# A gated mix of a long convolution and a shifted MLP: a new order of the steps behind the first 232, with new evacuation engines and ring buffers

## The chip, the cores and the metric

The kernel runs on one core of one Trainium2 chip. The metric is device time in microseconds. A core has TensorE (PE, with its weight loads shown apart as PEld), VectorE (DVE), ScalarE (ACT), GpSimd (POOL) and SyncE (SP), which here issues nearly all DMAs. Each engine works through its own queue in program order and waits on semaphores for the others.

## What is computed

S = 2048 positions of D = 640 channels, F = 1536. Cut to what matters:

```python
g = sigmoid((x * gate_w).sum(-1, keepdims=True))          # x = A_q
k_shift = sum over t < 4 of k_pad[:, t:t+S, :] * shift_k[:, 3-t]
kv = k_shift * v
y = irfft(rfft(kv, 2S) * rfft(ssm_k, 2S))[:S] + kv * ssm_D  # along the positions
a = x * y
h = gelu(layernorm(x) @ w1)
hs = shifted(h) @ w2        # four quarters of the channels shifted by 1, -1, 2, -2 positions
x1 = x + hs
b = x1 + gelu(layernorm(x1) @ w3) @ w4
return g * a + (1 - g) * b
```

## The kernel before, in words

The convolution is a two-stage Fourier transform on TensorE. **step1** (L423) multiplies kv (KV) and the filter (HT0) by a 64-point table; its PSUM banks are cast into a staging tile stg (L360 on ACT, L362 on DVE) and stored to DRAM scratch S_x (for kv) and S_h (for the filter). **gather** (L444) loads blocks of either, regrouped, into tiles ax. **step2** (L465) does the 32-point stage into XS and hs, **product** multiplies the spectra on DVE, **step3** (L512) transforms back into gs, stored to S_g (L523), **gin** loads it regrouped (L537), and **step4** (L893) does the last stage, with the gate and q applied (L897 to L907).

The MLP: **mlp1** (L707) into HT with gelu on ACT; **h_shift** on POOL; **w2** (L788), two PSUM banks of 320 columns for each of 16 tiles of positions, added to X on DVE (L791), with a square sum on ACT (L797); **x1_norm** normalizes four tiles into xn (L662 on ACT, L664 on DVE) and transposes them by DMA into x1t (L821); **w3** (L840) with gelu into gt (L844); **w4** (L867), added to X on DVE (L870); **store** (L855).

Steps are generators or lists of small pieces. The table ORDER names the 1099 pieces in the sequence in which they are emitted, "step1.HT0.2.VAVAAAAAAA:4" being piece 4 of step1 for block 2 of HT0; its letters say which evacuation goes to ACT (A) and which to DVE (V). Nothing else reorders the work, so ORDER sets each engine's queue. Tiles of a ring come from SLOTS: one digit for each tile in the order of allocation, saying which buffer it gets ("c": the 8 PSUM banks; "row": four buffers of 4 x 640 that stg, xn, gs, kn and q2 share; "ax": four for gather; "hp": four for hs). A new tile waits until everything that read its buffer's last tile is done, a DMA too.

Pieces that are tiled use a part of TensorE's rows or columns per matmul (step1, step2, step3, the gate); mlp1, w2, w3, w4 and step4 use all of them.

Of the kernel before, what the change touches and what calls it, by code (L numbers as in the profile page):

```python
# [41 lines left out]
def kernel(  # L42
# [24 lines left out]
        "c": "012345670124703510347205142356401723605162370514731057423671045261304732641374153670421350627413"  # L67
             "502634751264351270361427503164257364102546173045621537426107432715604371401362570164301257613045"
             "267236057416537621507362651374026372401534762501373150427102547535706432073125640736450750634127"
             "504763270415367204325170635147630125460327156034215760147362304167135620316425031672301402715320"  # L70
             "1724107361761423564023714053627501267420674256271306234",
# [807 lines left out]
    def step4(t1, ev):  # L879
# [32 lines left out]
        "open.L1.left:0 "  # L912
        "open.A2.right:0 "
        "consts0:0 "
        "load_x0.0:0 "
        "warm:0 "
        "load_x0.1:0 "
        "consts0:1 "
        "warm:1 "
        "warm:2 "  # L920
        "pow0:0 "
        "kv_alloc:0 "
        "k_load.3.AVA:0 "
        "f4_table:0 "
        "x_stats.0.VVVA:0 "
        "warm:3 "
        "k_load.3.AVA:1 "
        "x_stats.0.VVVA:1 "
        "load_x.1:0 "
        "x_stats.0.VVVA:2 "  # L930
        "k_load.3.AVA:5 "
        "x_stats.0.VVVA:3 "
        "x_stats.0.VVVA:4 "
        "x_stats.0.VVVA:5 "
        "x_stats.0.VVVA:6 "
        "warm:4 "
        "row_order:0 "
        "k_load.2.VAV:0 "
        "f1_table:0 "
        "x_norm.0.VVAA:0 "  # L940
        "x_norm.0.VVAA:1 "
        "f4_table:1 "
        "x_stats.1.VVVV:0 "
        "k_load.3.AVA:2 "
        "load_x.3:0 "
        "x_norm.0.VVAA:2 "
        "x_stats.1.VVVV:1 "
        "k_load.3.AVA:3 "
        "x_turn.0.AAA:0 "
        "k_load.3.AVA:6 "  # L950
        "k_load.2.VAV:5 "
        "load_w1.1:0 "
        "x_norm.0.VVAA:3 "
        "k_load.2.VAV:1 "
        "x_stats.1.VVVV:2 "
        "x_turn.0.AAA:1 "
        "x_stats.1.VVVV:3 "
        "x_turn.0.AAA:2 "
        "x_stats.1.VVVV:4 "
        "load_w1.0:0 "  # L960
        "x_stats.1.VVVV:5 "
        "x_stats.3.VVAA:0 "
        "k_load.3.AVA:4 "
        "x_norm.1.VVVV:0 "
        "x_turn.0.AAA:4 "
        "k_load.2.VAV:3 "
        "x_turn.0.AAA:3 "
        "x_turn.0.AAA:5 "
        "x_stats.3.VVAA:1 "
        "x_norm.1.VVVV:1 "  # L970
        "x_norm.1.VVVV:2 "
        "v_load.2:0 "
        "k_load.0.AAV:0 "
        "f1_table:1 "
        "mlp1.0.2:0 "
        "mlp1.0.3:0 "
        "x_norm.1.VVVV:3 "
        "v_load.0:0 "
        "k_load.1.AVV:0 "
        "k_load.2.VAV:6 "  # L980
        "mlp1.0.0:0 "
        "load_x.2:0 "
        "x_stats.3.VVAA:2 "
        "x_turn.1.VVV:0 "
        "x_turn.1.VVV:4 "
        "mlp1.0.1:0 "
        "x_stats.3.VVAA:3 "
        "x_turn.1.VVV:1 "
        "k_load.2.VAV:4 "
        "x_stats.3.VVAA:4 "  # L990
        "x_stats.3.VVAA:5 "
        "k_load.0.AAV:3 "
        "x_turn.1.VVV:5 "
        "mlp1.0.3:1 "
        "x_stats.3.VVAA:6 "
        "x_turn.1.VVV:2 "
        "v_load.3:0 "
        "x_turn.1.VVV:3 "
        "k_load.1.AVV:3 "
        "w1_mixed:0 "  # L1000
        "v_load.1:0 "
        "mlp1.0.0:1 "
        "x_stats.2.VVAA:0 "
        "mlp1.0.2:1 "
# [84 lines left out]
        "mlp1.3.3:0 "
        "tap.0.AVAA:3 "  # L1090
        "h_shift.0:2 "
        "tap.0.AVAA:5 "
        "tap.2.AVAA:8 "
        "h_shift.3:1 "
        "mlp1.3.2:0 "
        "tap.0.AVAA:4 "
        "tap.2.AVAA:6 "
        "tap.0.AVAA:1 "
        "mlp1.3.3:1 "
        "tap.0.AVAA:6 "  # L1100
        "tap.1.VAVA:0 "
        "tap.0.AVAA:7 "
        "tap.1.VAVA:5 "
        "tap.1.VAVA:1 "
        "tap.2.AVAA:4 "
        "mlp1.3.2:1 "
        "load_h.1:0 "
        "mlp1.2.2:0 "
        "tap.0.AVAA:8 "
        "tap.2.AVAA:1 "  # L1110
        "tap.1.VAVA:7 "
        "h_shift.1:1 "
        "tap.0.AVAA:2 "
        "load_h.3:0 "
        "mlp1.2.3:0 "
        "tap.1.VAVA:2 "
        "tap.1.VAVA:3 "
        "tap.2.AVAA:2 "
        "step1.KV.3.AAAVAVAAAV:9 "
        "tap.1.VAVA:8 "  # L1120
        "tap.1.VAVA:6 "
        "mlp1.2.2:1 "
        "mlp1.2.3:1 "
        "tap.1.VAVA:4 "
        "step1.KV.3.AAAVAVAAAV:11 "
        "step1.KV.3.AAAVAVAAAV:3 "
        "step1.KV.3.AAAVAVAAAV:10 "
        "step1.KV.3.AAAVAVAAAV:12 "
        "h_shift.0:3 "
        "step1.KV.3.AAAVAVAAAV:13 "  # L1130
        "step1.KV.3.AAAVAVAAAV:5 "
        "mlp1.2.4:0 "
        "step1.KV.3.AAAVAVAAAV:6 "
        "load_h.4:0 "
        "step1.KV.3.AAAVAVAAAV:0 "
        "step1.KV.3.AAAVAVAAAV:4 "
        "step1.KV.3.AAAVAVAAAV:14 "
        "h_shift.1:2 "
        "step1.KV.2.AVAVAVAAAA:6 "
        "z_rows:0 "  # L1140
        "z_rows:1 "
        "step1.KV.3.AAAVAVAAAV:2 "
        "step1.KV.3.AAAVAVAAAV:7 "
        "load_h.0:0 "
        "step1.KV.1.VAVAAAVVAA:0 "
        "step1.KV.3.AAAVAVAAAV:8 "
        "step1.KV.2.AVAVAVAAAA:8 "
        "step1.KV.3.AAAVAVAAAV:1 "
        "step1.KV.2.AVAVAVAAAA:3 "
        "z_rows:2 "  # L1150
        "mlp1.2.1:0 "
        "mlp1.2.1:1 "
        "h_shift.3:2 "
        "step1.KV.3.AAAVAVAAAV:16 "
        "step1.KV.1.VAVAAAVVAA:1 "
        "step1.KV.3.AAAVAVAAAV:15 "
        "mlp1.2.0:0 "
        "h_transpose.0.VV:2 "
        "step1.KV.2.AVAVAVAAAA:5 "
# [905 lines left out]
```

## Time and profile before

| | us |
|---|---|
| median of 3 runs (lowest to highest) | 227.55 (227.49 to 231.56) |
| the profiled execution | 227.13 |
| its span | 225.4 |
| PE busy | 217.8 (97%) |
| DVE busy | 183.7 (81%) |
| ACT busy | 171.4 (76%) |
| POOL busy | 38.1 (17%) |

The span is what the profiler saw of one execution; 1.7 us of the execution's time lie outside it. Busy matmuls overlap, since they are pipelined, so a matmul's own duration in the profile is longer than its share of the stream; the chain that ended last counts each stretch of time once. The granted clock is 1.00 in all stretches.

### The profile page before, as it was taken

How to read it: one execution, taken by the hardware profiler on the slowest of the kernel's cores; microseconds unless marked ns; L12 is line 12 of the kernel's file. 1: busy time of each engine (PE TensorE's matmuls, PEld its weight loads, DVE VectorE, ACT ScalarE, POOL GpSimd, SP SyncE). 2: the span in 40 equal slices, each digit the busy share in tenths (PEclk: the TensorE clock that was granted, in tenths of full speed). 3: DMA queues.
4: the chain of work that ended last, by engine and by line, in shares of the span. 5: the costliest groups of instructions: out<-in, count | busy, mean ns of one | idle time of the engine just before them, and what ended most of it. 6: DMA issues, size and time to landing. Idle time of an engine off the chain costs nothing.

```text
span 225.4 us, 6053 instructions
## 1 busy us (share of the span) xinstructions
PE 217.8 (97%) x2427; PEld 121.5 (54%) x2428; DVE 183.7 (81%) x447; ACT 171.4 (76%) x341; POOL 38.1 (17%) x91
## 2 busy tenths in 40 slices
PE   8989999899999999999999999999999999999994
PEld 2557455447846563345664444556533547657762
DVE  7898998868889969963899988989999841439994
ACT  4899988787999999999987597967988450266450
POOL 4247246816000431300600000000000000000000
PEclk9999999999999999999999999999999999999999
DMA  6999998892998999999989570690794879429914
GB/s 226 374 376 344 258 280 170 317 364 107 361 365 355 348 295 265 410 334 343 254 219 338 116 243 0 191 379 17 119 305 166 249 259 366 175 60 305 324 70 179
DMA packets 41770, 57.61 MB, mean 256 GB/s; under 512 B 18446, under 2 KB 34446, under 8 KB 41486
## 3 DMA queue, kind: packets, MB, share of 16 engines
q1 hardware_dynamic: 41166, 54.60, 75.4%
q0 software_dynamic: 576, 2.62, 3.1%
q8 instruction: 19, 0.31, 0.6%
q14 instruction: 9, 0.07, 0.1%
HBM read 34.93 MB, written 18.35 MB: 236 GB/s over the span
## 4 chain that ended last, share of the span: by engine, by line
PE 79%; DMA 9%; DVE 4%; ACT 4%; issue 1%; POOL 1%; SPq 0%; ACTq 0%
PE ps L840 24%; PE ps L867 23%; PE psw L788 7%; PE ps L465 5%; PE ps L893 4%; DMA X<-in_A_q_dram 4%; PE psm L707 4%; DMA xt<-xn 3%; PE psz L228 3%; PE ps L512 3%; PE ps L423 2%; PE pst L390 2%; DVE X L791 2%; ACT stg L360 2%; DMA S_x<-stg 2%; PE psk L590 1%
## 5 line engine op out<-in xcount | busy, mean ns | idle before, releaser
L840 PE MATMUL ps<-x1t,W 128*128 128x512 bf16 x240 | 56.1, 380 | 0.1
L867 PE MATMUL ps<-W,gt 128*128 128x320 bf16 (+2 forms) x383 | 55.1, 299 | 0.1
L867 PEld LDWEIGHTS <-gt 128*128 128x128 bf16 x384 | 36.2, 98 | 17.7 <-issue 3.0
L844 ACT ACTIVATE gt<-ps 128x512 bf16<-128x512 f32 x48 | 27.6, 609 | 19.0 <-PE ps L867 10.6
L840 PEld LDWEIGHTS <-W 128*128 128x128 bf16 x240 | 21.9, 98 | 28.7 <-issue 5.9
L360 ACT CAST stg<-ps 128x512 bf16<-128x512 f32 x55 | 28.6, 604 | 2.3 <-PE ps L423 2.0
L870 DVE SCALAR_TENSOR_TENSOR X<-ps,OMG,X 128x320 bf16<-128x320 f32 (+2 forms) x32 | 17.2, 547 | 11.9 <-PE ps L867 11.7
L707 PE MATMUL psm<-xt,WA 128*128 128x512 bf16 x100 | 23.4, 379 | 1.9 <-DMA WA<-in_B_w_dram 0.8
L360 ACT CAST gs<-ps 128x320 bf16<-128x320 f32 x41 | 15.6, 440 | 8.8 <-PE ps L512 4.8
L788 PE MATMUL psw<-WA,HT 128*128 128x320 bf16 x116 | 21.4, 300 | 0.0
L362 DVE CAST XS<-ps 128x512 bf16<-128x512 f32 x19 | 12.5, 684 | 6.7 <-PE ps L465 6.7
L362 DVE CAST stg<-ps 128x512 bf16<-128x512 f32 x25 | 15.8, 683 | 1.9 <-PE ps L423 1.9
L707 PEld LDWEIGHTS <-WA 128*128 128x128 bf16 x100 | 9.2, 97 | 12.9 <-DMA WA<-in_B_w_dram 1.0
L360 ACT CAST hs<-ps 128x512 bf16<-128x512 f32 x28 | 15.0, 605 | 1.4 <-PE ps L465 1.4
L791 DVE SCALAR_TENSOR_TENSOR X<-psw,X 128x320 bf16<-128x320 f32 x32 | 14.5, 487 | 1.6 <-PE psw L788 1.6
L897 ACT ACTIVATE y<-ps,GS 128x320 bf16<-128x320 f32 x22 | 10.4, 526 | 5.7 <-PE ps L893 3.5
L710 ACT ACTIVATE HT<-psm 128x512 bf16<-128x512 f32 x20 | 11.8, 617 | 3.6 <-PE psm L707 3.5
L788 PEld LDWEIGHTS <-HT 128*128 128x128 bf16 x116 | 10.7, 98 | 6.8 <-issue 3.1
L362 DVE CAST gs<-ps 128x320 bf16<-128x320 f32 x23 | 10.7, 484 | 2.4 <-PE ps L512 1.7
L797 ACT ACTIVATE jk<-X 128x640 bf16<-128x640 bf16 x16 | 12.2, 761 | 0.5 <-DVE X L791 0.4
L788 PE MATMUL psw<-WA,HM 128*128 128x320 bf16 x44 | 12.3, 299 | 0.0
L360 ACT CAST XS<-ps 128x512 bf16<-128x512 f32 x21 | 11.8, 607 | 0.5 <-PE ps L465 0.3
(151 smaller groups left out, 346.6 us busy)
## 6 DMA issues: line engine op xcount, KB each, us to landing
S_x<-stg SPq DMA_DIRECT2D x8, 640.0 KB, 4.3
S_h<-stg SPq DMA_DIRECT2D x8, 640.0 KB, 4.8
ax<-S_x SPq DMA_DIRECT2D x8, 640.0 KB, 5.9
ax<-S_h SPq DMA_DIRECT2D x8, 640.0 KB, 8.1
S_g<-gs SPq DMA_DIRECT2D x8, 640.0 KB, 3.6
W<-in_B_w_dram SPq DMA_DIRECT2D x2, 1920.0 KB, 9.1
kn<-in_A_k_dram SPq DMA_DIRECT2D x4, 640.0 KB, 6.9
E<-in_A_ssm_k_dram SPq DMA_DIRECT2D x5, 512.0 KB, 6.1
```

What stands on the lines that cost most here:

```text
L360: A.copy(out=dst, in_=src)
L362: V.tensor_copy(out=dst, in_=src)
L465: PE.matmul(ps[j][q:q + 32, lo - 512 * u:hi - 512 * u], lhsT=CMP[HALF[j], 8 * b + 4 * h + i, c, :], rhs=st[name, 2 * b + h][HALF[j], i, lo ...
L707: PE.matmul(ps[:].rearrange("p (a b) -> p a b", a=4), lhsT=W1N[:, k, 160 * u:160 * u + P] if u < 4 else W1M[:, k, :], rhs=xt[:, :, k, :], ...
L710: A.activation(out=st["HT"][:, 4 * c:4 * c + 4, u, :], in_=ps[:].rearrange("p (t b) -> p t b", t=4), func=ACT.Gelu_apprx_tanh)
L788: PE.matmul(ps[:], lhsT=h_tile(f, t1), rhs=W2P[:, f, o:o + W], start=(f == 0), stop=(f == 4))
L791: V.scalar_tensor_tensor(out=X1[:, t1, o:o + W], in0=box["ps"][:], scalar=1.0, in1=X[:, t1, o:o + W], op0=ALU.mult, op1=ALU.add, accum_out ...
L797: A.activation(out=jk[:], in_=X1[:, t1, :], func=ACT.Square, accum_out=S12[:, 1, t1:t1 + 1])
L840: PE.matmul(ps[:].rearrange("p (a b) -> p a b", a=4), lhsT=st["W3"][:, k, f * P:(f + 1) * P], rhs=xt[:, :, k, :], start=(k == 0), stop=(k ...
L844: A.activation(out=st["gt", c, f // 4][:, f % 4, :], in_=ps[:], func=ACT.Gelu_apprx_tanh)
L867: PE.matmul(ps[:], lhsT=st["gt", c, f // 4][:, f % 4, i * P:(i + 1) * P], rhs=st["W4"][:, f, o:o + w], start=(f == 0), stop=(f == FC - 1))
L870: V.scalar_tensor_tensor(out=X1[:, t1, o:o + w], in0=box["ps"][:], scalar=OMG[:, t1:t1 + 1], in1=X1[:, t1, o:o + w], op0=ALU.mult, op1=ALU ...
```

## The change

In ORDER the first 232 pieces stand in the same sequence (some letters of step1 differ among the last 25 of them); behind that the sequence is new. Both tables have the same 1099 pieces, apart from the letters. SLOTS is new from where the order differs: a tile of a ring gets the buffer that was free the longest. Functions and shapes are as they were.

```diff
     SLOTS = {
-        "c": "012345670124703510347205142356401723605162370514731057423671045261304732641374153670421350627413"
...
-        "row": "01230213021302320123012031203120310310303",
-        "gt": "012301031010231012301201",
+        "c": "012345670124703510347205142354610273415047321650235612703425671045376243506714203576127034516207"
...
+        "row": "01230213021302312013201012301231321302231",
+        "gt": "012301120323210301202301",
         "xt": "010101",
-        "gq": "0120201201021020120122102121021021",
-        "ax": "0123120312030213",
-        "hp": "01231302",
+        "gq": "01202012010210222012102111020",
+        "ax": "0123032103123012",
+        "hp": "01230312",
     }
...
     ORDER = (
...
-        "x1_norm.0.VVVV:0 "
...
+        "step1.HT0.1.AAAAAAAAAV:16 x1_norm.0.AVAV:0 w2.15:0 w2.15:1 x1_norm.0.AVAV:1 x1_norm.0.AVAV:2 w2.12:0 "
...
```

Of the letters: step1 has 30 pieces on DVE (25 before), step2 30 (31), step3 20 (23), step4 15 (10).

**DVE and ACT ahead of the first x1 transpose.** Before, DVE writes all four parts of xn for the first x1t in one go (psw2 are w2's banks, X the residual):

```order
L791 SCALAR_TENSOR_TENSOR X_102,S12_82<-psw2_1538,X_102 128x320
L791 SCALAR_TENSOR_TENSOR X_102,S12_82<-psw2_1579,X_102 128x320
L362 CAST stg_1602<-ps1_1587 128x4x128
L791 SCALAR_TENSOR_TENSOR X_102,S12_82<-psw2_1612,X_102 128x320
L791 SCALAR_TENSOR_TENSOR X_102,S12_82<-psw2_1621,X_102 128x320
L664 TENSOR_SCALAR xn_1650<-X_102,rn_1627 128x640 x4
L341 TENSOR_SCALAR n_1675<-m_1532 128x512
L275 TENSOR_SCALAR n_1675<-n_1675 128x512
```

Now ACT writes two of the four, among casts of step1 into stg:

```order
L797 ACTIVATE jk_1624,S12_82<-X_102 128x640
L360 CAST stg_1626<-ps1_1620 128x4x128
L360 CAST stg_1569<-ps1_1628 128x4x128
L360 CAST stg_1626<-ps1_1634 128x4x128
L360 CAST stg_1626<-ps1_1636 128x4x128
L360 CAST stg_1626<-ps1_1622 128x4x128
L662 ACTIVATE xn_1683<-X_102,rn_1680 128x640
L360 CAST stg_1549<-ps1_1692 128x4x128
L662 ACTIVATE xn_1683<-X_102,rn_1680 128x640
```

The four parts stood together on DVE; now two are on DVE and these two behind ACT's casts.

DVE, somewhat later in the changed kernel; stg_1778 has the ring buffer that xn_1683 had, and ps1_1772 the PSUM bank that the first w3 bank takes over:

```order
L791 SCALAR_TENSOR_TENSOR X_102,S12_82<-psw2_1734,X_102 128x320
L362 CAST stg_1769<-ps1_1765 128x4x128
L362 CAST stg_1778<-ps1_1772 128x4x128
L362 CAST stg_1769<-ps1_1780 128x4x128
L341 TENSOR_SCALAR n_1786<-m_1551 128x512
```

Two tiles are allocated in this ring behind xn_1683 up to the one that reuses its buffer (stg_1769, stg_1778); before, it were three behind xn_1650 (stg_1690, stg_1726, stg_1812).

**PE at the first gathers of h.** ax_2182 is gather h.6 and takes the buffer of ax_1915, gather x.0. The last matmul that reads ax_1915, now:

```order
L465 MATMUL ps2_2095<-ax_1915,CMP_80 32x512
L465 LDWEIGHTS CMP_80
L465 MATMUL ps2_2096<-ax_1915,CMP_80 32x512
L465 LDWEIGHTS CMP_80
L465 MATMUL ps2_2106<-ax_1832,CMP_80 32x512
```

and the first that reads ax_2182:

```order
L465 MATMUL ps2_2184<-ax_2167,CMP_80 32x256
L465 LDWEIGHTS CMP_80
L465 MATMUL ps2_2185<-ax_2167,CMP_80 32x256
L465 LDWEIGHTS CMP_80
L465 MATMUL ps2_2184<-ax_2182,CMP_80 32x256
L465 LDWEIGHTS CMP_80
```

Between the two lie 24 L867 matmuls and 32 L465 matmuls. Before, the third gather of h, ax_2240, took the buffer that PE had read up to here:

```order
L465 MATMUL ps2_2106<-ax_1680,CMP_80 32x384
L465 LDWEIGHTS CMP_80
L465 MATMUL ps2_2107<-ax_1680,CMP_80 32x384
L867 LDWEIGHTS gt_2002
L867 MATMUL ps4_2125<-W4_2090,gt_2002 128x320
```

and was first read here:

```order
L465 MATMUL ps2_2290<-ax_2180,CMP_80 32x512
L465 LDWEIGHTS CMP_80
L465 MATMUL ps2_2291<-ax_2180,CMP_80 32x512
L465 LDWEIGHTS CMP_80
L465 MATMUL ps2_2303<-ax_2240,CMP_80 32x512
L465 LDWEIGHTS CMP_80
```

with 48 L867 matmuls and 64 L465 matmuls between them.

**SP at the last pair of gathers.** Before, ax_2947 and ax_2988 (both from S_x) were the last pair:

```order
L523 DMA S_g_71<-gs_2489 128x4x640
L876 DMA q2_2723<-in_A_q_dram 128x2560
L444 DMA ax_2842<-S_h_69 128x4x640
L523 DMA S_g_71<-gs_2604 128x4x640
L444 DMA ax_2945<-S_h_69 128x4x640
L444 DMA ax_2947<-S_x_70 128x4x640
L444 DMA ax_2988<-S_x_70 128x4x640
L821 DMA_TRANSPOSE x1t_3222<-xn_2615 128x20x128
```

Now it is ax_2962 (x.4) and ax_3013 (h.5), the second from S_h, behind a pair of one of each; they take the buffers of ax_2695 and ax_2747:

```order
L444 DMA ax_2695<-S_h_69 128x4x640
L444 DMA ax_2747<-S_h_69 128x4x640
L523 DMA S_g_71<-gs_2572 128x4x640
L444 DMA ax_2863<-S_x_70 128x4x640
L444 DMA ax_2958<-S_h_69 128x4x640
L444 DMA ax_2962<-S_x_70 128x4x640
L444 DMA ax_3013<-S_h_69 128x4x640
L523 DMA S_g_71<-gs_2824 128x4x640
```

One store of gs stood between the two h gathers of the last four; now the four stand together, and h.5 is the last of them.

More of the change, by code (lines that the diff above doesn't have):

```diff
@@ L911 @@
     ORDER = (
[L912 to L932, printed above, removed]
@@ L1149 @@
[L1149 to L1159, printed above, removed]
-        "w2.0:0 "
-        "mlp1.2.4:1 "
-        "mlp1.2.0:1 "
-        "w2.15:0 "
-        "t2_table:1 "
-        "step1.KV.2.AVAVAVAAAA:4 "
-        "step1.KV.1.VAVAAAVVAA:3 "
@@ L1398 @@
-        "w3.0.10:0 "
-        "step1.HT0.0.VAAVVAVAVV:14 "
-        "step1.HT0.0.VAAVVAVAVV:13 "
-        "w3.0.7:1 "
-        "step2.x.0.VAVVAVAAVA:9 "
-        "step2.x.3.AVVVVVAAVA:3 "
-        "w3.0.10:1 "
-        "step1.HT0.0.VAAVVAVAVV:10 "
-        "step2.x.0.VAVVAVAAVA:6 "
-        "w3.0.4:0 "
-        "step1.HT0.0.VAAVVAVAVV:11 "
-        "gate:0 "
-        "step2.x.0.VAVVAVAAVA:11 "
-        "w2.15:4 "
-        "step2.x.0.VAVVAVAAVA:8 "
-        "step2.x.3.AVVVVVAAVA:0 "
-        "x1_norm.1.VVAA:0 "
@@ L1415 @@
-        "w3.0.4:1 "
-        "step1.HT0.1.VVAAAAAAVA:16 "
-        "step2.x.0.VAVVAVAAVA:7 "
-        "step2.x.3.AVVVVVAAVA:4 "
-        "w2.10:4 "
-        "step2.x.3.AVVVVVAAVA:1 "
-        "x1_norm.1.VVAA:1 "
-        "gate:1 "
-        "w3.0.3:0 "
-        "x1_norm.1.VVAA:2 "
-        "step2.x.3.AVVVVVAAVA:5 "
-        "step2.x.3.AVVVVVAAVA:6 "
-        "w3.0.11:0 "
-        "step2.x.3.AVVVVVAAVA:7 "
-        "step2.x.0.VAVVAVAAVA:10 "
-        "w3.0.11:1 "
-        "w3.0.3:1 "
-        "step1.HT0.1.VVAAAAAAVA:15 "
@@ L1433 @@
-        "x1_norm.1.VVAA:3 "
-        "w3.0.5:0 "
-        "step2.x.3.AVVVVVAAVA:12 "
-        "w2.11:4 "
-        "step2.x.3.AVVVVVAAVA:9 "
-        "w3.0.1:0 "
-        "w3.0.5:1 "
-        "step1.HT0.0.VAAVVAVAVV:15 "
-        "step2.x.3.AVVVVVAAVA:10 "
-        "step1.HT0.0.VAAVVAVAVV:16 "
-        "gate:2 "
-        "w3.0.0:0 "
-        "w3.0.2:0 "
-        "w2.14:4 "
-        "step2.x.3.AVVVVVAAVA:2 "
-        "step2.x.3.AVVVVVAAVA:14 "
-        "step2.x.3.AVVVVVAAVA:11 "
-        "w3.0.0:1 "
@@ L1560 @@
-        "x1_norm.2.AVVV:5 "
-        "w3.1.2:1 "
-        "product.1:3 "
-        "product.1:4 "
-        "product.6:0 "
-        "step3.7.AAAAAVAV:6 "
-        "w4.0:3 "
-        "w3.1.9:1 "
-        "step2.h.0.AAVAAAAAVA:4 "
-        "step3.7.AAAAAVAV:9 "
-        "gather.h.2:0 "
-        "step3.7.AAAAAVAV:7 "
-        "product.6:1 "
-        "w3.1.1:0 "
-        "step3.1.VAAVVVAA:5 "
-        "step3.1.VAAVVVAA:7 "
-        "x1_norm.3.AVAA:1 "
-        "w3.1.8:0 "
-        "x1_norm.3.AVAA:2 "
@@ L1652 @@
-        "step2.h.1.AAAAVAVAAA:9 "
-        "step2.h.1.AAAAVAVAAA:14 "
-        "w4.5:1 "
-        "w4.4:1 "
-        "step2.h.1.AAAAVAVAAA:0 "
-        "gather.h.5:0 "
-        "gather.x.5:0 "
-        "step3.6.AAVVAVAA:4 "
-        "step2.h.1.AAAAVAVAAA:10 "
-        "step2.h.1.AAAAVAVAAA:13 "
-        "step2.h.1.AAAAVAVAAA:11 "
-        "product.3:0 "
-        "w4.6:0 "
-        "step3.6.AAVVAVAA:5 "
-        "gather.x.4:0 "
-        "w3.2.3:0 "
-        "w4.6:1 "
-        "step3.6.AAVVAVAA:8 "
@@ L2008 @@
-        "store.8:1 "
-        "close.L2:0 "
-        "close.C:0 "
[170 rows of a table added]
     ).split()
```

974 lines of the change are left out of this document (4 added, 970 removed), and 169 rows, old and new, of the table ORDER.

## The prediction

> **What bounds the kernel now.** I read the page first, then the time table by stretches, PE's waits, and the chain that ended last.
>
> ```profile
> PE 217.8 (97%) x2427; PEld 121.5 (54%) x2428; DVE 183.7 (81%) x447; ACT 171.4 (76%) x341; POOL 38.1 (17%) x91
> PE   8989999899999999999999999999999999999994
> PE 79%; DMA 9%; DVE 4%; ACT 4%; issue 1%; POOL 1%; SPq 0%; ACTq 0%
> ```
>
> PE is the bound, and it has no holes behind the first quarter. The table by stretches says how small they are (stretch, length, PE, PEld, DVE, ACT, POOL, then granted clock and DMA):
>
> ```profile
> 30.00:60.00 30.00, 28.80 (x465) 17.15 (x454) 24.94 (x60) 24.50 (x47) 15.69 (x34) 1.00 0.77 258
> 60.00:90.00 30.00, 29.86 (x212) 16.57 (x210) 26.55 (x89) 28.61 (x55) 4.81 (x11) 1.00 1.01 329
> 90.00:120.00 30.00, 30.00 (x398) 15.73 (x398) 22.36 (x43) 28.76 (x61) 5.90 (x18) 1.00 1.01 317
> 120.00:150.00 30.00, 30.00 (x359) 14.83 (x358) 27.58 (x46) 23.49 (x48) 0.00 (x0) 1.00 0.62 190
> 150.00:180.00 30.00, 29.99 (x404) 14.74 (x401) 28.43 (x43) 22.71 (x52) 0.00 (x0) 1.00 0.64 183
> ```
>
> Busy matmuls overlap, so I test this with the chain, whose pieces do not (start, length, what):
>
> ```profile
> 95.12 0.34 PE ps L465 x8
> 99.25 0.56 PE ps L465 x24
> 113.29 3.37 PE ps L867 x24
> 119.53 2.16 PE ps L840 x10
> 121.68 0.41 PE ps L512 x16
> 122.09 2.27 PE ps L840 x10
> 148.72 1.19 PE ps L840 x5
> 212.21 1.63 PE ps L867 x12
> 219.00 2.34 PE ps L867 x10
> 221.36 1.02 DVE X L870 x2
> ```
>
> Twelve L867 matmuls take 1.63 us and ten L840 take 2.16, the same wherever they stand: PE streams from about 54 us to 221. The same matmuls remain after the change, so what a new order can win there is the holes (1.2 + 0.14 us in the table, part of them ahead of the changed steps) and the small price of alternating. Ten L840 matmuls cost 2.27 us behind a tiled step (L512), 2.16 behind an untiled one; with the same again on entry a tiled stretch costs 0.1 to 0.2 us. That is about 2 us in all, under 1% of the time. What it can lose is open upwards: each matmul that comes to its data or its PSUM bank too early.
>
> **The change part by part.** I set the new order of each engine beside these durations and asked at each place: who is late?
>
> *Removed.* Counted in the order, PE's stretches of tiled steps behind the gate matmuls fall from 44 to 41: three by 0.1 to 0.2 us, -0.3 to -0.6, taken as -0.5. Work is otherwise the same; in step4 five evacuations go from ACT to DVE, priced at the end.
>
> *The first transpose of x1.* It now waits for ACT.
>
> ```profile
> 44.31 3.59 ACT stg L360 x7
> L662 ACT ACTIVATE xn<-X,rn x6: 907/909/962, 108.8 to 157.7; 128x640 bf16<-128x640 bf16 x6
> 47.76 0.62 ACT L723 COPY zr<-psz 128x512 f32<-128x512 f32 x1
> 78.09 4.40 SPq L821 DMA_TRANSPOSE x1t<-xn  x1
> x1t<-xn SPq DMA_TRANSPOSE x1, 6.3
> DMA to landing us min/median/max: 4.9/5.1/6.3
> 87.07 1.24 PE L840 MATMUL ps<-x1t,W 128*128 128x512 bf16 x5
> S_x<-stg SPq DMA_DIRECT2D x8, 640.0 KB, 4.3
> DMA to landing us min/median/max: 2.9/4.3/4.8
> ```
>
> The rows: seven casts on ACT back to back (0.51 us each); one normalization on ACT (0.91); where ACT's queue stands as the orders part (47.76); the transpose's issue (78.09), its own landing 6.3 us later, and landings of all four transposes; the first w3 matmul (87.07); landings of S_x stores, twice. Before, DVE wrote all of xn, and 87.07 - (78.09 + 6.3) = 2.7 us were to spare. Now ACT writes two of the four parts, and from zr on it has ahead of the last part, by the order, 36 casts into stg (18.4), 3 other 512-wide evacuations (1.5), 3 transposed copies, a table load, a sine and 6 squares (together some 9), and the two parts themselves (1.8): about 30 us. 47.8 + 30 = 77.8 if ACT never idles. It will, by the same count: stg_1338 takes the ring buffer that a store to S_x left at about 54.7, and ACT is there at 57.6, so with 4.3 to landing it waits 1.4; stg_1507 takes one stored at 65.2, ACT is there at 68.2, 1.3 more; and 0.9 for PE. So the transpose goes out at 81.4 and lands 4.9 to 6.3 later, 86.3 to 87.7. PE comes to its first w3 matmul two w2 banks earlier (10 matmuls, 1.4) and with two more pairs of step1 (0.5) behind it: 87.07 - 0.9 = 86.2. There is more behind the same landing: the buffer of this xn goes to stg_1778, DVE's cast into it stands still until the transpose has read it, and the bank that this cast empties is the one w3 wants. Cast 0.68: the bank is free at 87.0 to 88.4. PE is late by 0.8 to 2.2 us; if stores land in 2.9 and ACT never idles 0; if in 4.8, 3. I take 2.0, near the transpose that has the same traffic around it (6.3). Queued behind the transpose on SP are a store to S_h and gather x.6; SP is held 4.4 us, to about 85.8, x.6 then lands 5.7 to 7.7 later (rows below), 91.9 to 93.9, and is wanted 6.6 us of PE work behind the first w3 matmul, 92.8 and with the stall 94.8: just covered by that work, at nothing; up to 1 if the stall is not there.
>
> *The gathers of h.* Where the first four h gathers take over ring ax from x, three wait for step2's last x units, now placed together right ahead of the w4 matmuls.
>
> ```profile
> ax<-S_h SPq DMA_DIRECT2D x1, 640.0 KB, 8.2
> 105.08 0.36 SPq L444 DMA_DIRECT2D ax<-S_h  x1
> ax<-S_h SPq DMA_DIRECT2D x1, 640.0 KB, 5.3
> 112.45 0.84 PE L465 MATMUL ps<-ax,CMP 64*32 64x256 bf16 x32
> W<-in_B_w_dram SPq DMA_DIRECT2D x1, 1920.0 KB, 9.6
> ```
>
> Issue at 100.3 lands in 8.2; issue at 105.08 in 5.3, and its matmuls stand in the row of 112.45: 7 us of PE work hid it. Now PE has between the release of the buffer and the first use of gather h.6 two units (0.56 - 0.34 = 0.22 each), 24 L867 matmuls (3.37) and one unit (0.34): 4.15 us. Late by 5.3 - 4.15 = 1.15 up to 8.2 - 4.15 = 4.05. Gather h.1 goes out 0.45 later and is wanted some 2.1 later: lead 5.85 against 8.2 behind a neighbour, 2.3. The waits overlap; I take 2.4 for the place. Queued on PE behind it is everything, so the whole goes to the end. Load of W4 (9.6) has as much lead as before.
>
> *The last pair of gathers* (x.4, h.5) goes out as h.2 and h.3 are used up.
>
> ```profile
> ax<-S_x SPq DMA_DIRECT2D x1, 640.0 KB, 5.7
> ax<-S_x SPq DMA_DIRECT2D x1, 640.0 KB, 7.7
> 142.35 0.46 SPq L444 DMA_DIRECT2D ax<-S_h  x1
> ax<-S_h SPq DMA_DIRECT2D x1, 640.0 KB, 8.0
> ```
>
> First and second of the pair at 83 landed in 5.7 and 7.7, the second h gather at 142.35 in 8.0. PE's cover is 5 L840, a L512 unit, 5 L840, a L512 and a L465 unit together, 12 L867, a L512 unit, 5 L840: 1.19 + 0.41 + 1.19 + 0.63 + 1.74 + 0.41 + 1.19 = 6.8, less 0.55 until the second is issued: 6.2. Second of the pair is h.5, and it is wanted first. Late by 1.5 to 2.0, or not at all if it lands like a first; taken 1.4, since little else is in flight there.
>
> *The end.* Among DVE's last instructions ahead of the final two (221.36 above) now stand three w4 results of 0.55 where one stood, two of them left from earlier, so the final two start when DVE is free instead of when PE is done: 0.5 (0 to 0.6).
>
> *Sum*, against the profiled execution's own 227.13 us (span 225.4): -0.5 + 2.0 + 2.4 + 1.4 + 0.5 = +5.8, 232.9. The median of the runs, 227.55, is 0.42 above that execution: 233.3.
>
> **The rivals.** (a) *The transfers land in time*: not slower. One mechanism: a gather's landing. If h.6 lands within 4.15 us and h.5 within 6.2, both stalls are gone, and with S_x stores in 2.9 us ACT does not idle and the first goes too: 227.55 - 0.5 + 0.5 = 227.6. For it: the kernel's store of 640 KB landed in 2.9 once. Against it: no gather of the same size landed under 5.3. The Trainium skill, DMA: Bandwidth & Descriptors, section Anatomy of one DMA (SWDGE path), gives 2.0 us plus bytes over 436 GB/s, an estimate of 3.5 us for 640 KB, by which h.6 and h.5 would be in time. These are issued by SP, which is not the path of that fit, and the rows of 5.3 to 8.2 disagree with it. (b) *Only one or two of the stalls come*: +2 to +4.4, 229.5 to 232; for it: a PE that is late once comes later to the next place that hangs on ACT or DVE (not to the gathers, whose issue hangs on PE itself). (c) *Stalls breed more*: a store that PE's delay pushes into another gather, ring waits elsewhere on ACT, +10: 237.5. (d) *PE is not the bound and the new order packs better*, over 2% faster, below 223: the page's waits give it under 2 us, so it would have to come from PE itself. The Trainium skill, Perfetto Trace Analysis, section Identifying the Most-Contended Engine, warns that matmul busy time misleads and asks for weight-load busy, here 54%; the chain's even 136 and 216 ns a matmul say that PE streams all the same.
>
> **How the numbers follow.** Forecast (all three stalls, near their values; 232 to 236) 0.50, (a) 0.18, (b) 0.20, (c) 0.10, (d) 0.02. About 2% is what a measurement of this kernel can tell from no change; 2% slower is 232.1. So slower is 0.50 + 0.10 = 0.60, same (a) and (b), 0.38, faster 0.02. The sum of all low ends is -0.6 + 0 + 1.2 + 0 + 0 = +0.6, of all high ends -0.3 + 3 + 4.1 + 2.0 + 0.6 = +9.4 (237.0). The range reaches from (a) to the price of (c): 227.8 to 237.5.
>
> **What would show it.** Right: PE waiting for a DMA into ax for 1 to 4 us near 110 and again near 150; DVE or ACT idle behind DMA x1t<-xn just ahead of the first L840; ACT waits for S_x stores of over 1 us in all, where the list of waits has one of 0.2 now:
>
> ```profile
> ACT stg L360 <- DMA S_x<-stg: 0.2, 1, 0.2
> ```
>
> The times per matmul stay as they are. Wrong: no wait of PE for a DMA behind 60 us, gathers that land in under 4.15, or a first L840 at or before 86.2. If the stalls come but the time does not rise, the bound on what the stream can win is wrong.

## The result and the profile after

The changed kernel takes 230.62 us, the median of six runs (229.52 to 232.19), against 227.78 for the kernel before: ratio 1.0117, 95% interval 1.0079 to 1.0154. It is slower by 2.8 us, a little over 1%, and the interval excludes no change. Forecast were 233.3, that is 5.8 more. Some executions lie over 1.5% above the fastest of their version; the ratios leave these out, the medians do not. The profiled execution took 232.19 us (span 230.4) and is the slowest of its six, so what it shows must not be taken for the median; a second profile (first experiment) stands beside it below.

From the page of the changed kernel: busy time of the engines, PE's slices, and the chain that ended last by engine.

```profile
PE 218.1 (95%) x2428; PEld 121.5 (53%) x2428; DVE 186.6 (81%) x448; ACT 169.0 (73%) x335; POOL 39.7 (17%) x91
PE   8989999999999998999899999899999998999894
PE 52%; DMA 21%; DVE 16%; ACT 6%; issue 2%; POOL 1%; SPq 0%; DVEq 0%
```

PE has the same work and less of the span. Where there were nines from the first quarter to the end, there are eights now, one each near 87, 110, 149, 194 and 214 us, and DMA holds 21% of the chain instead of 9%. PE's list of waits (engine, line, what it waited for; us in total, times, longest) names them, and ACT's and DVE's lists have three more on ring row, two of them for stores to S_x:

```profile
PE ps L465 <- DMA ax<-S_h: 1.6, 2, 1.0
PE ps L893 <- DMA gin<-S_g: 1.1, 1, 1.1
PE ps L893 <- DVE X L870: 1.0, 1, 1.0
PE ps L840 <- DVE stg L362: 1.0, 1, 1.0
ACT stg L360 <- DMA S_x<-stg: 2.1, 4, 0.8
DVE stg L362 <- DMA S_x<-stg: 2.0, 2, 1.7
DVE stg L362 <- DMA x1t<-xn: 1.4, 1, 1.4
```

The chain (start, length, what) shows how four of PE's waits come about:

```profile
81.81 4.82 DMA x1t<-xn
86.72 0.70 DVE stg L362
87.47 2.32 PE ps L840 x10
...
105.36 4.76 DMA ax<-S_h
110.17 0.52 PE ps L465 x24
...
141.55 7.31 DMA ax<-S_h
148.91 0.85 PE ps L465 x40
...
182.25 1.75 ACT gs L360 x5
184.02 5.79 DMA S_g<-gs
190.44 3.80 DMA gin<-S_g
194.25 1.52 PE ps L893 x10
```

The first is the forecast place with the forecast way (transpose, DVE's cast, bank); the second and third are gathers h.6 and h.5, also forecast; the fourth, step4's first load behind the last store to S_g, was not.

**A measure that the start does not disturb.** The order is new only behind piece 232. I measure from the last gate matmul (L719, unchanged) to the last w4 matmul (L867), the stretch. A line's row has first and last start of its matmuls; here before, then the changed kernel:

```profile
L719 PE MATMUL psz<-xt,GWR x20: 379/379/390, 46.4 to 47.3; 128*32 128x512 bf16 x20
L867 PE MATMUL ps<-W,gt x383: 219/299/379, 104.9 to 221.8; 128*128 128x320 bf16 x180, 128*128 128x512 bf16 x6, 128*128 128x128 bf16 x6
```

```profile
L719 PE MATMUL psz<-xt,GWR x20: 379/379/390, 45.8 to 46.7; 128*32 128x512 bf16 x20
L867 PE MATMUL ps<-W,gt x384: 219/299/379, 105.6 to 226.8; 128*128 128x320 bf16 x180, 128*128 128x512 bf16 x6, 128*128 128x128 bf16 x6
```

221.8 - 47.3 = 174.5 us before, 226.8 - 46.7 = 180.1 now: in these two executions 5.6 us were lost, nearly the 5.8 that were forecast; the parts show below that this nearness is luck. The same rows for the profiles that follow (e3 is read only in one place):

| kernel | last L719 | first and last L867 | stretch | median of its runs | ratio to before |
|---|---|---|---|---|---|
| before | 47.3 | 104.9, 221.8 | 174.5 | 227.78 |  |
| before again | 48.6 | 106.6, 223.4 | 174.8 | 229.39 | 1.0014 |
| changed | 46.7 | 105.6, 226.8 | 180.1 | 230.62 | 1.0117 |
| changed again (e1) | 48.4 | 105.7, 226.0 | 177.6 | 231.24 | 1.0103 |
| e2 gathers | 48.5 | 106.0, 225.8 | 177.3 | 231.38 | 1.0114 |
| e4 tail letters | 47.5 | 105.0, 225.7 | 178.2 | 232.26 | 1.0175 |
| e5 buffer for xn | 48.2 | 104.9, 224.8 | 176.6 | 231.30 | 1.0084 |
| e6 gin1 | 48.1 | 105.6, 225.8 | 177.7 | 230.98 | 1.0086 |
| e7 gin1 and letters | 48.5 | 105.6, 227.4 | 178.9 | 232.80 | 1.0171 |
| e8 gin0 | 48.9 | 108.2, 226.8 | 177.9 | 232.67 | 1.0141 |
| e9 gin1 and q2 | 48.4 | 106.0, 225.4 | 177.0 | 230.73 | 1.0062 |
| e10 all | 48.2 | 105.0, 222.0 | 173.8 | 227.69 | 0.9940 |
| e11 all but gin0 | 48.3 | 105.0, 223.2 | 174.9 | 229.31 | 0.9992 |

The kernel before ran beside all of them; its median was 228.66 beside e1 to e4, 229.18 to 229.37 later, so versions of different rows are better compared by the ratio than by the median. The stretch is that of one execution each.

### The profile page after: what moved, and what is told of

Its sections match the earlier page's. It is cut to its first block, busy times and chain, and to the rows that moved or that the text cites. A ratio compares the mean times of both kernels' runs of the same rounds, so it can differ in the third digit from the quotient of the medians.

```text
span 230.4 us, 6050 instructions
## 1 busy us (share of the span) xinstructions
PE 218.1 (95%) x2428; PEld 121.5 (53%) x2428; DVE 186.6 (81%) x448; ACT 169.0 (73%) x335; POOL 39.7 (17%) x91
## 4 chain that ended last, share of the span: by engine, by line
PE 52%; DMA 21%; DVE 16%; ACT 6%; issue 2%; POOL 1%; SPq 0%; DVEq 0%
PE ps L840 21%; PE ps L867 11%; DMA xt<-xn 6%; DMA ax<-S_h 5%; PE ps L465 4%; PE psw L788 4%; DVE b L685 3%; ACT stg L360 3%; DMA S_g<-gs 3%; DVE X L907 2%; PE ps L512 2%; PE psm L707 2%; PE pst L390 2%; DMA x1t<-xn 2%; DVE q L903 2%; PE ps L893 2%
## 5 line engine op out<-in xcount | busy, mean ns | idle before, releaser
L840 PE MATMUL ps<-x1t,W 128*128 128x512 bf16 x240 | 56.1, 380 | 1.0 <-DVE stg L362 1.0
L867 PE MATMUL ps<-W,gt 128*128 128x320 bf16 (+2 forms) x384 | 55.4, 299 | 0.0
L867 PEld LDWEIGHTS <-gt 128*128 128x128 bf16 x384 | 36.2, 98 | 17.8 <-issue 3.3
L840 PEld LDWEIGHTS <-W 128*128 128x128 bf16 x240 | 22.0, 98 | 28.7 <-issue 5.9
L360 ACT CAST stg<-ps 128x512 bf16<-128x512 f32 x50 | 26.5, 607 | 3.2 <-DMA S_x<-stg 2.1
L870 DVE SCALAR_TENSOR_TENSOR X<-ps,OMG,X 128x320 bf16<-128x320 f32 (+2 forms) x32 | 16.7, 544 | 10.4 <-PE ps L867 10.4
L897 ACT ACTIVATE y<-ps,GS 128x320 bf16<-128x320 f32 x17 | 8.3, 525 | 21.6 <-PE ps L893 19.6
L362 DVE CAST stg<-ps 128x512 bf16<-128x512 f32 x30 | 19.5, 684 | 5.1 <-DMA S_x<-stg 2.0
L360 ACT CAST gs<-ps 128x320 bf16<-128x320 f32 x44 | 16.7, 445 | 7.1 <-PE ps L512 4.3
L360 ACT CAST hs<-ps 128x512 bf16<-128x512 f32 x28 | 15.7, 620 | 2.8 <-PE ps L465 2.8
L362 DVE CAST XS<-ps 128x512 bf16<-128x512 f32 x18 | 11.7, 684 | 3.9 <-PE ps L465 3.8
L903 DVE SCALAR_TENSOR_TENSOR q<-ps,GS,q 128x320 bf16<-128x320 f32 x15 | 7.9, 546 | 8.2 <-PE ps L893 8.1
L360 ACT CAST XS<-ps 128x512 bf16<-128x512 f32 x22 | 12.6, 606 | 1.7 <-PE ps L465 1.7
L465 PE MATMUL ps<-ax,CMP 64*32 64x128 bf16 (+3 forms) x512 | 12.0, 299 | 1.6 <-DMA ax<-S_h 1.6
L362 DVE CAST gs<-ps 128x320 bf16<-128x320 f32 x20 | 9.1, 486 | 4.2 <-PE ps L512 2.3
```

Source lines behind the costliest of these rows:

```text
L360: A.copy(out=dst, in_=src)
L362: V.tensor_copy(out=dst, in_=src)
L465: PE.matmul(ps[j][q:q + 32, lo - 512 * u:hi - 512 * u], lhsT=CMP[HALF[j], 8 * b + 4 * h + i, c, :], rhs=st[name, 2 * b + h][HALF[j], i, lo ...
L840: PE.matmul(ps[:].rearrange("p (a b) -> p a b", a=4), lhsT=st["W3"][:, k, f * P:(f + 1) * P], rhs=xt[:, :, k, :], start=(k == 0), stop=(k ...
L867: PE.matmul(ps[:], lhsT=st["gt", c, f // 4][:, f % 4, i * P:(i + 1) * P], rhs=st["W4"][:, f, o:o + w], start=(f == 0), stop=(f == FC - 1))
L870: V.scalar_tensor_tensor(out=X1[:, t1, o:o + w], in0=box["ps"][:], scalar=OMG[:, t1:t1 + 1], in1=X1[:, t1, o:o + w], op0=ALU.mult, op1=ALU ...
```

## Experiments

**e1: the changed kernel again.** No edit.

> The changed kernel once more, nothing edited: a second profile and five more rounds. Theory: its extra time is the sum of PE's waits at six places (first w3 matmul 1.1 us, gather h.6 0.8, gather h.5 1.0, step4's first load 1.3, DVE's backlog in step4 1.2, two ring waits near 53 us 1.1), less 0.7 of a shorter stream; those that hang on a transfer vary from run to run, so in a median run (230.6 us, 1.5 less than the one profiled) one or two of the transfer waits (87, 110, 149, 194 us) are smaller by 1.5 us together, while DVE's wait near 214 stays at 1.0 to 1.4. Rival: the transfer waits stay as they are (sum 4.2) and it is the last 25 us, bound by DVE, that differ.

PE's waits behind 60 us:

```profile
PE ps L893 <- DMA gin<-S_g: 2.4, 2, 1.5
PE ps L840 <- DVE stg L362: 0.9, 1, 0.9
PE ps L465 <- DMA ax<-S_h: 0.6, 1, 0.6
```

The stretch is 2.5 us shorter than in the first profile, and the page shows where: gather h.5 came in time (nothing at 149 instead of 1.0) and the waits of ACT and DVE for stores to S_x fell from 4.1 us to 0.6, so that PE lost nothing on ring row near 53 us: from the last L719 to the first L867 it is 57.3 us instead of 58.9. The waits at 87, 110, 194 and 214 came back. The theory holds in part: of the four transfer waits (87, 110, 149, 194) one vanished and another grew by 0.4, 0.7 us less together instead of 1.5, and the larger part of the difference is the ring wait near 53, which the theory had not among those that vary. The ratio, 1.0103 (1.0055 to 1.0151), agrees with the first. In the quieter of the two executions the change thus costs 177.6 - 174.5 = 3.1 us, in the other 2.5 more. The wait at 214, one for DVE X L870 in the first profile, is one for gin here; from e1's chain:

```profile
207.25 6.48 DMA gin<-S_g
213.87 0.99 PE ps L893 x6
```

**Before again.**

> The kernel before once more, nothing edited, for a second profile. What the reorder changes lies between the last gate matmul (L719) and the last matmul of all; that stretch took 174.5 us in the first profile of before, 180.1 and 177.6 in the two of the changed kernel, while the unchanged part ahead of L719's last matmul ended anywhere from 46.7 to 50.1 us. Theory: PE streams in the stretch, so it repeats: 174.2 to 174.9, whatever the start does. Rival: the stretch of before varies too, by 1 us or more, and part of the 3.1 us is luck.

174.8: the theory. Against this profile the 3.1 us are 2.8, and they are the change's.

**e2: a fifth buffer for gathers h.6 and h.5.**

```diff
-        "ax": "0123032103123012",
+        "ax": "0123402103123041",
```

with gather.h.6 ahead of gather.h.7 in the order and gather.h.5 behind gather.h.4.

> Gathers h.6 and h.5 get a fifth buffer of ring ax and go out one piece earlier in SP's queue; everything else as in the changed kernel. Theory: PE's waits for DMA ax at 110 and 149 us (0.8 + 1.0 in the profiled run) are gone and the end moves by as much: 228.8 to 229.4 against 230.6. Rival 1 (the time is given back): PE comes to step4's first load and to DVE's backlog earlier and waits there instead, 230.2 to 230.6, with waits at 194 and 214 us grown by over 1 us. Rival 2: the earlier gathers crowd the other two of their pair and those come late instead, waits for ax remain over 1 us.

No wait for ax is left on PE's list:

```profile
PE ps L893 <- DMA gin<-S_g: 2.6, 2, 1.4
PE ps L840 <- DVE stg L362: 1.0, 1, 1.0
```

The cure works where it is applied, and the stretch falls by 0.3 only: 0.6 won at 110, and 0.1 and 0.2 more paid at the first w3 matmul and at step4's loads. The time does not show it at all (231.38, ratio 1.0114); runs of one kernel differ by more. Neither the forecast gain in time nor a rival's return of over 1 us is there: against e1's profile there were 0.6 to win, not the 1.8 of the first.

**e3: the first normalization all on DVE again.**

```diff
-        "x1_norm.0.AVAV:0 ... x1_norm.0.AVAV:6"
+        "x1_norm.0.VVVV:0 ... x1_norm.0.VVVV:6"
```

> The first normalization of x1 wholly on DVE again, as in the kernel before (letters VVVV for AVAV), all else as in the changed kernel. Theory (ACT is what makes the transpose late): the transpose goes out 1 to 3 us before 81.8, PE's wait at the first w3 matmul (1.1 us at 87) falls to 0.2 or less, the time to 229.5 (-1.1). Rival: DVE, which is as loaded there, carries the 1.3 us more just as late, or the wait of its cast for the buffer comes in the same place: the wait stays at 0.8 to 1.2 and the time within 0.3 of 230.6.

The time is 231.63 (ratio 1.0108), the wait for DVE stg ahead of the first L840 1.0 us, as in the changed kernel. The profiled execution took 235.89 us, 4 more than the median, so only the place itself is read, in L719's row and the timelines of SP and of the engine that writes the last part of xn, first e1, then e3:

```profile
80.87 0.96 ACT L662 ACTIVATE xn<-X,rn 128x640 bf16<-128x640 bf16 x1
81.86 3.00 SPq L821 DMA_TRANSPOSE x1t<-xn  x1
```

```profile
L719 PE MATMUL psz<-xt,GWR x20: 379/379/389, 49.2 to 50.1; 128*32 128x512 bf16 x20
83.97 0.44 DVE L664 TENSOR_SCALAR xn<-X,rn 128x640 bf16<-128x640 bf16 x1
84.44 3.00 SPq L821 DMA_TRANSPOSE x1t<-xn  x1
```

From L719 the transpose goes out 81.86 - 48.4 = 33.5 us later with ACT and 84.44 - 50.1 = 34.3 with DVE. This execution of e3 also lost time on ring row near 53 us (DVE waited 1.0 us for a store to S_x), so a mark close to the place is safer: PE was ready for the first w3 matmul at 87.57 - 0.85 = 86.7 in e1, 4.9 us behind the transpose's issue, and at 90.13 - 0.98 = 89.2 in e3, 4.7 behind it. In the changed kernel ACT does write the last part, 0.4 us behind DVE's last; but DVE alone, with the same queue of w2 results and casts ahead, is no earlier. So, against the prediction, the letters do not decide it; what is left is the place in the order. The rival was right.

**e5: a buffer of its own for the first xn.**

```diff
-                xn = slot(ring, [P, 4, D], BF16, "xn", "row", ROW)
+                xn = pool("C").tile([P, 4, D], BF16, name="xn", tag="ax4", bufs=1) if c == 0 else \
+                    slot(ring, [P, 4, D], BF16, "xn", "row", ROW)
```

(one digit of SLOTS["row"] goes with it).

> The first x1 normalization writes to a buffer of its own, so that DVE's next cast into ring row (stg) no longer stands behind the transpose's read; letters, order and all other buffers as in the changed kernel. Theory: PE is late at the first w3 matmul by the way over the cast (transpose read, then 0.7 us of cast, then the bank); without it PE waits only for the transpose itself, which lands within 0.3 us of PE's arrival: the wait at 87 falls from 1.0 to 0.1 to 0.4, and the stretch from L719 on from 177.6 to 176.9. Rival: the transpose's landing is the limit, and the wait stays over 0.8.

PE's waits behind 60 us (line numbers from 817 on are one higher in this kernel):

```profile
PE ps L894 <- DMA gin<-S_g: 1.7, 2, 1.4
...
PE ps L841 <- DMA x1t<-xn: 0.3, 1, 0.3
```

0.9 becomes 0.3: two thirds of the wait were DVE's cast standing behind the transpose's read of its ring buffer, the rest the transpose. The stretch is 176.6, 1.0 shorter, where the theory had 0.7 (176.9); 0.6 of it lie here, and in this execution the waits for gin were 0.7 shorter too and that for ax 0.1 longer. The time is 231.30, ratio 1.0084 (1.0020 to 1.0147).

**e4: five step4 evacuations back to ACT.**

```diff
-        step4.10.AV  step4.11.VA  step4.12.AV  step4.13.VV
+        step4.10.AA  step4.11.AA  step4.12.AA  step4.13.AA
```

(with a fourth buffer "gq").

> Five evacuations of step4 (places 10, 11, 12 and both of 13) go back to ACT, as in the kernel before, with a fourth small buffer for their copies; order as in the changed kernel. Theory: DVE saves 0.22 us on each, 1.1 us in its backlog from 207 us on, PE's wait for DVE near 214 (1.2 us) falls to 0.3 or less and the time to 229.6 (-1.0). Rival: DVE is not what the end waits for, PE's queue is full to the end anyway (last matmul follows PE's stream): within 0.3 of 230.6.

A miss, and a badly placed test: these four places read gin1 and come behind 214 us, so they cannot lighten DVE ahead of it. The time is 232.26, ratio 1.0175 (1.0113 to 1.0237). The wait stayed and one for ACT came on top:

```profile
PE ps L893 <- DVE X L870: 1.0, 1, 1.0
PE ps L893 <- ACT y L897: 0.5, 1, 0.5
```

**e6: gin1 in a free buffer.** W3's buffer is free only after the last w3 matmul.

```diff
-            ... name="gin1", tag="W3") if q == 1 else \
+            ... name="gin1", tag="RT") if q == 1 else \
```

> The load gin1 gets the buffer of HT0/XS (tag RT), free since the last product, instead of that of W3, free only after the last w3 matmul (205 us); order as in the changed kernel. Theory: at 214 us two things end together, gin1's landing (213.7) and DVE's backlog (213.9), so that taking one away wins 0.0 to 0.3 us: the wait of 1.05 stays at 0.8 to 1.1, now for DVE X L870 alone. Rival: gin1 is what PE waits for, and the wait falls under 0.3.

The rival was right: no wait at 214 is on the list.

```profile
PE ps L465 <- DMA ax<-S_h: 1.8, 2, 1.5
PE ps L893 <- DMA gin<-S_g: 1.2, 1, 1.2
PE ps L840 <- DVE stg L362: 1.0, 1, 1.0
```

DVE's and PE's timelines of this run say why "DVE X L870" was never the cause:

```profile
213.63 3.70 PE L893 MATMUL ps<-gin,F 128*128 128x320 bf16 x26
214.19 0.55 DVE L870 SCALAR_TENSOR_TENSOR X<-ps,OMG,X 128x320 bf16<-128x320 f32 x1
```

PE passed at 213.63 while that DVE instruction started at 214.19. In the profile of the changed kernel it merely ended closest to PE's start. In e1's chain the way led over gin1, whose load ends at 207.25 + 6.48 = 213.73, just ahead of PE; the DVE instruction ended there at 213.93, behind PE's start at 213.87.

The stretch did not fall (177.7), since gather h.5 took 7.80 us this time and cost 1.5. And the end moved away: the last q2 load waits for a buffer that step4's places 0 to 3 hold, and DVE works through to the end behind it.

From the chain:

```profile
141.17 7.80 DMA ax<-S_h
...
213.08 4.83 DMA q<-in_A_q_dram
```

Span less last L867 is 230.0 - 225.8 = 4.2 us against 3.6 (229.6 - 226.0) in e1. The size is that of the prediction's term for DVE at the end, but not the way: DVE waited 0.5 us for this load, and e9 below, with DVE's work unchanged and the load early, is back at 3.6. The time is 230.98, ratio 1.0086 (1.0062 to 1.0110).

**e7: gin1 as in e6, and four evacuations of places 6 and 7 on ACT.**

```diff
-        step4.6.VV  step4.7.VV
+        step4.6.AA  step4.7.AA
```

> gin1 as in the run before (buffer of HT0/XS), and four evacuations of step4 that stand in DVE's backlog ahead of 214 us (places 6 and 7) go to ACT, with three more small buffers for the copies. Theory (two limits at once): with both gone the wait at 214 falls from 1.05 to 0.3 or less, the stretch from 177.6 to 176.8. Rival: DVE's final instructions set the end, what PE wins it waits for later: the stretch stays within 0.3 of 177.6.

Worse: 232.80, ratio 1.0171 (1.0153 to 1.0190). DVE was not the limit, and now ACT is, with w3's last gelu and the copies in one queue.

```profile
PE ps L893 <- ACT gt L844: 1.0, 1, 1.0
```

**e9: gin1 as in e6, and the last q2 in a buffer of the finished gathers.**

```diff
-        q2 = slot(ring, [P, 4, D], BF16, "q2", "row", ROW)
+        q2 = pool("C").tile([P, 4, D], BF16, name="q2", tag="ax0", bufs=1) if c == 3 else \
+            slot(ring, [P, 4, D], BF16, "q2", "row", ROW)
```

> gin1 in the buffer of HT0/XS as in the run with gin1 alone, and the last load of q2 (load_q.3) in a buffer of the finished gathers instead of the one that step4's places 0 to 3 hold until 213 us. With gin1 alone PE's wait at 214 was gone but DVE waited for this load until 217.9 and ended 1.2 us behind PE's last matmul start (0.7 before), span less last matmul 4.2 us instead of 3.6. Theory: both limits gone, no PE wait at 214 and 3.6 to 3.7 us from last matmul to the end; the stretch 176.5 plus what h.5's landing takes (0 to 1.5). Rival: DVE is bound by its own work from 206 us on, whatever is loaded when: it still ends the kernel, 4.0 us or more behind the last matmul.

No wait at 214, and span less last L867 is 229.0 - 225.4 = 3.6: the end's two limits are gone. The stretch is 177.0, where the theory had 176.5 and more; step4's first load took 1.6 of it, h.5 0.3. The time is 230.73, ratio 1.0062 (1.0033 to 1.0091).

**e8: more work ahead of step4's first load.**

```diff
-        "... gin.0.2:0 step4.1.VA:3 w4.11:1 w4.9:3 ...  step4.4.VA:6 w4.8:0 w3.3.0:1 w4.8:1 ..."
+        "... gin.0.2:0 w4.8:0 step4.1.VA:3 w4.11:1 w4.9:3 w4.8:1 ...  step4.4.VA:6 w3.3.0:1 ..."
```

(the PSUM banks in SLOTS["c"] follow the new order).

> One group of 12 w4 matmuls (w4.8, first half) is moved from behind step4's first block to right ahead of it; all else as in the changed kernel. Theory: step4's first load (gin0) is late by a fixed chain, last gs cast, store to S_g (6 us), gin0 (3.8 us), against too little PE work (about 10 us); 1.63 us more work ahead of it takes the wait at 194 from 1.3 to 1.7 down to 0.3 or less, and the stretch from L719 to the last matmul from 177.6 to 176.3. Rival: PE then comes earlier to gin1 and DVE's backlog and waits there instead: the wait at 214 grows by 1 us or more and the stretch stays at 177.2 to 177.8.

At step4's first block PE no longer waits (PE's timeline):

```profile
194.31 1.79 PE L863 MATMUL ps<-W,gt 128*128 128x320 bf16 x12
195.94 1.52 PE L889 MATMUL ps<-gin,F 128*128 128x320 bf16 x10
```

From first to last w4 matmul it is 226.8 - 108.2 = 118.6 us against 120.3 in e1, and the wait at 214 stays at 0.9 to 1.0: nothing is given back. But the time is 232.67 (ratio 1.0141, 1.0098 to 1.0184) and the stretch 177.9. The profiled execution lost about 2 us ahead of the first w4 matmul (59.3 us from L719 to there, 57.3 in e1). Those lie near 55 us, on ring row:

```profile
DVE stg L358 <- DMA S_x<-stg: 2.5, 1, 2.5
PE pst L386 <- DVE stg L358: 1.0, 1, 1.0
```

So the place is confirmed and the time contradicts; that the other runs lost theirs on ring row too is not shown. The last run tests the move again.

**e10: all cures together** (the edits of e2, e5, e8 and e9).

> All of the cures together, order otherwise as in the changed kernel: gathers h.6 and h.5 in a fifth buffer, first xn in a buffer of its own, gin1 and the last q2 in free buffers, the w4 group ahead of step4. Theory (the loss is the sum of those five waits, and the new order's stream itself is 0.7 us shorter): PE waits 0.5 to 1.2 us in all behind 60 us, the stretch from L719 to the last matmul is 172.8 to 173.6 against 174.5 and 174.8 of before, and the time is 0.990 to 0.997 of before. Rival: curing one wait moves PE into the next, the stretch stays over 175 and the ratio over 1.0.

227.69 us, median of twelve runs; ratio to before 0.994 (0.9911 to 0.9969). Behind 60 us PE's list has one entry:

```profile
PE ps L837 <- DMA x1t<-xn: 0.2, 1, 0.2
```

The stretch is 173.8: 3.8 under e1, where the waits on the list were 3.9 in all, and 0.7 to 1.0 under the two profiles of before. The waits and the time are as the theory had them or better (0.2 against 0.5 to 1.2 us; 0.990 to 0.997), the stretch is 0.2 over its range (172.8 to 173.6). This version is 0.6% faster than the kernel before, with the same 41 stretches of tiled steps as the changed kernel.

**e11: all but e8's move.**

> All cures but one: as the run with all of them, with the w4 group back behind step4's first block. Theory: only the wait for gin0 returns, 1.3 to 1.8 us near 190, the stretch from L719 to the last matmul is 175.1 to 175.7 (173.8 with all), the time 1.3 to 1.8 us over that of all cures, about equal to before (0.998 to 1.003). Rival: the w4 move was worth nothing or did harm (alone it timed 232.7, no better than the changed kernel, while its profile showed the wait gone): the stretch stays at 173.5 to 174.2 and the ratio at 0.994 or under.

```profile
PE ps L895 <- DMA gin<-S_g: 1.1, 1, 1.1
```

The wait for gin0 is back, the stretch 174.9 (1.1 more, a little under the forecast), the time 229.31, ratio 0.9992 (0.9959 to 1.0024). e10 and e11 were not run side by side; by the ratios they are 0.5% or 1.2 us apart, and the intervals just touch. With the rest quiet, the move is worth what its place shows; why e8 alone timed so high stays open beyond its one profile.

## Why the prediction was right in direction and twice too large

The step that failed is the pricing of the stalls. The places, the ways and PE's cover were mostly right, but each term was one number for a landing, taken in the middle or at the slow end of the rows: gather h.6 at 2.4 us cost 0.6, the first transpose at 2.0 cost 1.0 and 0.9, gather h.5 at 1.4 cost 1.0 and 0, and DVE at the end at 0.5 cost nothing. That is 6.3 forecast and 2.6 or 1.5 measured. Two waits that the list did not have at all, for step4's loads gin0 and gin1, added 2.1 and 2.4. That the total came out at half of the forecast and not at a quarter is luck, and so is the 5.6 of the first profile.

| step | forecast | first profile | e1 |
|---|---|---|---|
| shorter stream | -0.5 | -0.7 to -1.0 (e10) | the same |
| first x1 transpose | 2.0 | 1.0 | 0.9 |
| gather h.6 | 2.4 | 0.6 | 0.6 |
| last pair, h.5 | 1.4 | 1.0 | 0 |
| DVE at the end | 0.5 | 0 | 0 |
| step4's first load gin0 | none | 1.1 | 1.5 |
| gin1 | none | 1.0 | 0.9 |
| ring row, S_x stores | none on PE | about 1.5 | 0 |

The rows of waits come from the list, the last from the 58.9 and 57.3 us under e1. The columns add up to 5.2 to 5.5 and 2.9 to 3.2 us, against 5.6 and 3.1 in the stretch.

*Shorter stream.* Right in sign and near in size: e10 has the new order nearly without its waits, and its stretch is 0.7 to 1.0 under before's. The tiled stretches did fall from 44 to 41; how much of the gain is theirs and how much are the holes of before, no run separates.

*The first transpose.* The place, the way and the times were right: forecast issue 81.4, bank free 87.0 to 88.4; measured 81.81 and 87.4. (The times of ACT's queue in the prediction add up to 30.7, put down as about 30.) PE comes at 87.47 - 1.0 = 86.5, forecast 86.2. The term was mis-sized: I took 2.0 from 0.8 to 2.2, near the row of 6.3 us for a landing, and it landed in 4.82. The reason given, ACT's share, does not hold, since DVE alone is as late (e3), and that the issue came out right is partly luck; that DVE's cast is stuck behind the transpose's read is shown (e5).

*Gather h.6.* The cover was right: forecast 4.15 us, and PE's wait began 110.17 - 0.6 - 105.36 = 4.2 us after the issue. The landing was not: 4.76 us, under the lower end of 5.3. To take 2.4 was to take a landing of 6.5, near the middle between two rows; of 2.4 there were 0.6. By the fit in the Trainium skill, DMA: Bandwidth & Descriptors, section Anatomy of one DMA — SWDGE (gpsimd) path, an estimate is 3.5 us and no wait; the trace has 4.76, and PE did wait.

*The last pair.* Cover forecast 6.2, measured 148.91 - 1.0 - 141.55 = 6.4; landing 7.31 in the first profile, 7.80 in e6, 6.59 in e9, and in time in e1. A cover in the middle of a spread of landings costs nothing in one execution and 1.5 in another; one number for it was the mistake.

*DVE at the end.* It cost nothing. The end lies 3.6 us behind the last w4 matmul's start before (225.4 - 221.8), in the changed kernel (230.4 - 226.8) and in e10, where PE comes on time (225.6 - 222.0). The 4.2 of e6 came from the late q2 load (e9).

*What was missed.* The part by part list followed the ring ax and the first transpose, and step4's change only as letters ("in step4 five evacuations go from ACT to DVE"). Taking letters back won nothing (e7; those of e4 come too late to tell). The order did it. Before (SP's and PE's timelines):

```profile
185.58 3.04 SPq L537 DMA_DIRECT2D gin<-S_g  x3
...
194.70 5.56 PE L840 MATMUL ps<-x1t,W 128*128 128x512 bf16 x25
200.09 5.33 PE L893 MATMUL ps<-gin,F 128*128 128x320 bf16 x38
...
210.14 2.06 PE L893 MATMUL ps<-gin,F 128*128 128x320 bf16 x14
```

The last parts of gin0 were out by 188.6 and step4 began at 200.09, with 25 w3 matmuls (5.6 us) between the w4 block and it; places 0 to 7 of step4 read gin0, 8 to 13 gin1. Now five stand there, and step4's first block comes while its load still has cast, store (5.79), queue (0.6) and load (3.80) to go. Gin1 cannot start before w3's last matmul: from there to its first use PE had 210.14 - 200.3 = 9.9 us of other work; in e1 w3 ends at 205.4 and PE is ready for gin1 at 213.87 - 0.9 = 213.0, 7.6 us later. Together that is 2.1 us in the first profile and 2.4 in e1, about half of what the four forecast terms were too large by (3.7 and 4.8).

The signs named beforehand: a wait of PE for ax near 110 came, but under the 1 us set as its lower end; one near 150 came in some executions; DVE idle behind x1t<-xn came (1.4); ACT's waits for S_x stores came in the first profile (2.1) and hardly in the second (0.6). The time falls into rival (b)'s span, but not by its way: no stall spared another (e10 and e11 add up place by place), the stalls were small, and two unforeseen ones filled half the gap.

Open: why stores to S_x land late near 53 us in some executions (the changed kernel's first, e8) and not in others, with the same instructions ahead. Nothing was run on it. In these two, the DMA engines moved less from 8 to 4 us ahead of the last L719 than in the other ten profiles of this order (252 and 269 GB/s against 315 to 371) and more in the last 2 us ahead of it (396 and 349 against 237 to 327), as if earlier transfers had slipped beside the first stores; that this is the cause is not shown.

## What to carry to other kernels

When an order changes, list every transfer that moves against its first reader and its last writer, from the first store to the last load, and compare cover with landing for each; here the two places left out made about half of PE's waits. Where the cover lies inside the spread of landings, give the wait a range and not a value; even the row with the like traffic around it was no safe price here (6.3 taken for the first transpose, 4.82 measured). Judge cures place by place in the trace, from a mark that the change does not touch: single cures of 0.3 to 1.6 us drowned in a spread of 2 us between runs, while all of them together took the ratio to the kernel before from 1.0103 to 0.994, some 3.7 us.

## What the runs showed that was not expected

The first part ends anywhere from 46.7 to 50.1 us after the start (last L719 in the rows and table above), in the changed kernel alone and with the same instructions there, at a mean granted clock of 0.997 to 1.000: as much spread as the change's effect. The releaser that a profile names for a wait can be the wrong one of two that end within 0.2 us of each other: "DVE X L870" at 214 in the first profile was gin1's landing (e6). And the landing of the same gather, h.5, left PE nothing to wait for in e1 and took 7.31 and 7.80 us in two other executions, for 1.0 and 1.5 us of waiting.
